# Reordering the opening and the first hand-over of a fused attention and MLP kernel on one Trainium2 core

## The chip, the core and the metric

The kernel runs on one core of one Trainium2 chip. The metric is device time in microseconds (us). Profiles are single executions; "span" is the profiled time from first to last instruction, some 2 us less than the timed figure. Every run here was in the fast state. A verdict compares the mean of one kernel's fast runs with the mean of the other's of the same rounds; that ratio is given with its 95% interval and is not quite the ratio of the medians also quoted. In the profiles PE is TensorE, DVE VectorE, ACT ScalarE, POOL GpSimd and SP SyncE.

## The reference, cut to what matters

```python
# attention part: batch 4, 8 heads, 768 positions, head dim 32, state 16, chunks
y_intra = einsum('bhij,bhjd->bhid', (C @ B.T) * exp(cum_i - cum_j) * causal, x)
y_inter = einsum('bhin,bhnd->bhid', C, state) * exp(cum_i)
state   = decay_full * state + sum_j(B_j x_j * decay_from_j)
# MLP part: 3072 tokens, 256 -> 2048 -> 256
h = y @ w_in ; g = h * clip(h + 3, 0, 6) / 6 ; out = g @ w_out
```

The kernel works in six chunks of 128 positions. The opening computes chunk 0's attention output. Chunk 0's MLP (the first MLP, writing `h`, then the output products, writing `o`) is followed by five denser stages. The weights arrive in a raw 64-bit form and are decoded by ScalarE and VectorE in eight parts, most of them while the first MLP runs.

Some names recur. `cb`, the scores, is the product of C and B; `bT` is B transposed and `csT` is C transposed and scaled; the state sum adds a chunk to the state, and the middle state (`mid`) stands between the chunk's two halves. The hand-over is the passage from chunk 0's output products to the next stage, and the lead is that stage's first products, put ahead of the rest.

## The kernel before

Each name is an instruction stream per engine; a call appends to all of them in program order. In the trace each engine's instructions follow in that order (PE, kernel before: C's transposes at 9.79 us, B's at 12.61, scores at 13.91, state sum at 16.47, products at 18.16).

```python
def turn_ps(c, j):                       # banks for the transposes of C (j=0), B (j=1)
    if c + j == 1: return ps.tile(..., tag="f1")
    if c * j == 1: return ps.tile(..., tag="f2")
    return ps_o.tile(..., tag="o")
def first_eto():
    e_ps = ps.tile([P, NB, HT], FP32, name="e_ps", tag="f0")   # ...
def scores(c):                           # C B^T into cb (f0..f3), then the state sum
    # ... 32 cb matmuls
    for b in range(NB):
        for q in range(NQ):
            for a in range(2):           # both halves of the state sum, at once
                nc.tensor.matmul(out=sps[c][a][...], ...)
def multiply(c):
    nc.scalar.copy(out=adds[c], in_=sps[c][1])
    for q in range(NQ):
        nc.vector.tensor_tensor(out=Ls[c]..., in0=Ls[c]..., in1=cbs[c][q], op=ALU.mult)
        if q == 1: ...                   # the middle state, from sps[c][0]
# a buffer of the MLP stages shares its tag with the output copy 'ob':
up = ffn.tile([P, 2, 2 * P], FP32, name="up", tag="ob", bufs=2)

# opening, in program order (cut)
diff(0, *range(NB)); load_w(1); load_w(2)
weights(0, ...)                          # decode of weight part 0
store_rows(); first_eto(); diff(1, 2, 3)
turn_c(0, t_ps); weights(0, 1); turn_b(0); fade_c(0, t_ps)
diff(1, 1); scores(0); diff_mask(1, 0); diff(1, 0)
multiply(0); mix(0)                      # mix: chunk 0's products, then from_state
by_token(); keep(0); weights(1, 2); renew(0); weights(1, 3)
# first MLP, then first_out(b, i): 16 units of 8 recorded PE products; (i, b) =
#   (2, 1): scores(1), multiply(1), renew(1)   (3, 0): results(1)   (3, 2): lead(1, 0)
```

## Time and profile before

| | value |
|---|---|
| time, median of 3 runs | 366.31 us |
| span of the profiled run | 364.3 us |
| PE busy | 347.9 us (96%) |
| PE idle in the opening (10 to 26 us) | 2.2 + 1.4 + 4.0 us |
| clock at half | 22.08 to 28.91 us |
| first MLP product / first output product | 25.75 / 54.87 us |

A line of a timeline has the start, the time to the group's end, engine and source line, what is written from what, shapes, the count, and in brackets the idle time ahead and what ended it; "issue" means that the profile shows nothing that was waited for. The lines of the kernel before stand in the prediction.

### The profile page before, as it was taken

The page shows a single profiled execution, that of the slowest core. Times are in us where ns is not written, and L with a number is a line of the kernel's source. Part 1 is how long each engine was busy: PE and PEld are TensorE (multiplying, and loading weights), DVE is VectorE, ACT ScalarE, POOL GpSimd, SP SyncE. Part 2 cuts the span into 40 slices and gives each one's busy share as a digit, 9 for nine tenths or more (in the row PEclk, how much of TensorE's full clock was granted, in tenths as well). Part 3 has the DMA queues.
Part 4 walks back from the last instruction along what each step waited for, and adds up shares of the span by engine and source line. Part 5 has one row for each costly group of instructions (what it writes and reads, how often), then busy time and mean ns, then how long its engine had stood idle before and what let it go on. Part 6 is the DMA issues. An engine that isn't in the chain of part 4 may idle for free.

```text
span 364.3 us, 9338 instructions
## 1 busy us (share of the span) xinstructions
PE 347.9 (96%) x3936; PEld 299.5 (82%) x3936; DVE 222.7 (61%) x429; ACT 176.2 (48%) x386; POOL 136.6 (38%) x138
## 2 busy tenths in 40 slices
PE   6659999989999999999999999999999999999996
PEld 2444448878788999888999888999888999888996
DVE  7729999976588625588436488435488411588111
ACT  5528888457556470376380376380367110376100
POOL 3200000072198922069822059820058800058800
PEclk9979999999999999999999999999999999999999
DMA  9975989900845025451016452000000000000000
GB/s 168 158 282 154 112 267 162 172 3 31 180 61 78 5 60 119 69 87 19 2 40 139 69 87 19 2 4 31 29 2 1 2 4 31 30 3 0 2 29 31
DMA packets 78538, 24.97 MB, mean 69 GB/s; under 512 B 69088, under 2 KB 74880, under 8 KB 77984
## 3 DMA queue, kind: packets, MB, share of 16 engines
q1 hardware_dynamic: 78496, 24.37, 36.0%
q8 instruction: 31, 0.51, 0.6%
q14 instruction: 11, 0.09, 0.1%
HBM read 21.07 MB, written 3.29 MB: 67 GB/s over the span
## 4 chain that ended last, share of the span: by engine, by line
PE 86%; DVE 4%; DMA 3%; ACT 2%; issue 2%; SPq 2%; DVEq 0%; ACTq 0%
PE ob L721 18%; PE oa L721 17%; PE even L610 16%; PE odd L610 12%; PE h L568 8%; PE o L662 7%; DMA xt<-in_x_dram 3%; PE y L546 3%; PE y L462 2%; SPq L92 1%; PE cb L485 1%; PE y L493 1%; DVE odd L639 1%; DMA out_dram<-ob 1%; DVE up L626 1%
## 5 line engine op out<-in xcount | busy, mean ns | idle before, releaser
L707 POOL TENSOR_TENSOR s<-gT 128x512 f32<-128x512 f32 x20 | 26.4, 1321 | 90.6 <-DVE gT L651 90.6
L610 PE MATMUL even<-ts,w_sum 128*128 128x256 f32 x160 | 48.3, 384 | 0.0
L625 ACT COPY even<-odd 128x512 f32<-128x512 f32 x40 | 23.1, 576 | 48.5 <-PE odd L610 46.3
L646 ACT ACTIVATE gT<-odd,half 128x512 f32<-128x512 f32 x40 | 27.5, 687 | 36.4 <-DVE odd L639 36.4
L610 PE MATMUL odd<-yT,w_in 128*128 128x256 f32 x160 | 41.1, 379 | 0.0
L721 PE MATMUL oa<-w_out,gT 128*128 128x128 f32 x320 | 38.9, 277 | 0.0
L721 PEld LDWEIGHTS oa<-w_out,gT 128*128 128x128 f32 x320 | 38.1, 192 | 0.9
L721 PE MATMUL ob<-w_out,s 128*128 128x128 f32 x320 | 37.4, 275 | 0.0
L721 PEld LDWEIGHTS ob<-w_out,s 128*128 128x128 f32 x320 | 36.5, 192 | 0.0
L610 PEld LDWEIGHTS even<-ts,w_sum 128*128 128x128 f32 x160 | 29.8, 190 | 5.5 <-ACT up L632 1.8
L651 DVE SCALAR_TENSOR_TENSOR gT<-gT,odd 128x512 f32<-128x512 f32 x40 | 27.5, 687 | 9.9 <-ACT gT L646 9.8
L610 PEld LDWEIGHTS odd<-yT,w_in 128*128 128x128 f32 x160 | 30.1, 190 | 3.9
L361 ACT ACTIVATE L<-L,cum_n 128x64 f32<-128x64 f32 x128 | 31.2, 339 | 0.0
L626 DVE COPY up<-odd 128x256 f32<-128x256 f32 x40 | 17.0, 424 | 22.1 <-ACT even L625 17.7
L721 PE MATMUL ob<-t,gT 128*128 128x128 f32 x240 | 30.3, 279 | 0.0
L646 ACT ACTIVATE gT<-even,half 128x512 f32<-128x512 f32 x40 | 27.7, 693 | 4.4 <-PE even L610 4.4
L651 DVE SCALAR_TENSOR_TENSOR gT<-gT,even 128x512 f32<-128x512 f32 x40 | 27.1, 678 | 4.4 <-ACT gT L646 4.4
L568 PE MATMUL h<-yT,w_in 128*128 128x512 f32 x64 | 29.3, 620 | 0.0
L721 PEld LDWEIGHTS ob<-t,gT 128*128 128x128 f32 x240 | 27.9, 192 | 1.1 <-issue 0.5
L662 PE MATMUL o<-w_out,gT 128*128 128x256 f32 x128 | 28.7, 381 | 0.0
L662 PEld LDWEIGHTS o<-w_out,gT 128*128 128x128 f32 x128 | 24.1, 190 | 3.7 <-issue 0.5
L379 POOL TENSOR_TENSOR tmp<-state,eto 128x256 f32<-128x256 f32 x5 | 3.1, 621 | 64.1 <-ACT eto L365 64.0
(126 smaller groups left out, 618.0 us busy)
## 6 DMA issues: line engine op xcount, KB each, us to landing
raw<-in_moe_w_in_dram SPq DMA_DIRECT2D x4, 1024.0 KB
raw<-in_moe_w_out_dram SPq DMA_DIRECT2D x4, 1024.0 KB
L<-cum_d SPq DMA_DIRECT2D x8, 512.0 KB
xt<-in_x_dram SPq DMA_DIRECT2D x6, 512.0 KB
out_dram<-res SPq DMA_DIRECT2D x20, 128.0 KB
B<-in_B_dram SPq DMA_DIRECT2D x6, 256.0 KB
eto<-cum_e SPq DMA_DIRECT2D x20, 64.0 KB
C<-in_C_dram SPq DMA_DIRECT2D x3, 256.0 KB
```

The costliest lines, as they stand in the source:

```text
L361: nc.scalar.activation(Ls[c][:, b, h], Ls[c][:, b, h], AF.Exp, bias=cum_n[:, c, g:g + 1])
L462: nc.tensor.matmul(out=ys[c][a, q // 2][d0:d0 + 2 * D, b], lhsT=state[pair, b], rhs=csT[pair, b, HALF[a]], start=(a == 0 and b == 0), stop ...
L546: nc.tensor.matmul(out=ys[c][a, u][d0:d0 + D, b], lhsT=xt[rows, b * NH + h], rhs=Ls[c][rows, b, h], start=(a == 1 and b == 0), stop=True, ...
L568: nc.tensor.matmul(out=h.rearrange("p r i -> p (r i)"), lhsT=w_in[:, j, f * P:(f + 1) * P], rhs=yTs[k][:, j].rearrange("p b i -> p (b i)") ...
L610: nc.tensor.matmul(out=bank[:, r], lhsT=lhsT, rhs=rhs, start=start, stop=True, skip_group_check=True)
L625: nc.scalar.copy(out=even, in_=odd[:, 1:2].to_broadcast([P, 2, 2 * P]))
L626: nc.vector.tensor_copy(out=up[:, 1], in_=odd[:, 0])
L646: nc.scalar.activation(gTs[k][:, f], h.rearrange("p r i -> p (r i)"), AF.Relu, bias=half, scale=1.0 / 6.0)
L651: nc.vector.scalar_tensor_tensor(out=g, in0=g, scalar=1.0, in1=h.rearrange("p r i -> p (r i)"), op0=ALU.min, op1=ALU.mult)
L662: nc.tensor.matmul(out=o[:, b % 2], lhsT=gTs[0][:, f, b * P:(b + 1) * P], rhs=w_out[:, f], start=(f == 0 and b % 2 == 0), stop=True, skip_ ...
L707: nc.gpsimd.tensor_tensor(out=o, in0=p_, in1=q_, op=op)
L721: nc.tensor.matmul(out=bank[:, slot], lhsT=lhs[:, j], rhs=rhs[:, j], start=(clear and j == 0), stop=True, skip_group_check=True)
```

## The change

It has two intents. In the opening, PE's wait for B is to be filled with chunk 1's differences and with idle products meant to keep the clock up, and half of the state sum goes behind the products so that they can start sooner. At the hand-over, chunk 1's scan moves one output unit on to cover a wait.

```diff
-        e_ps = ps.tile([P, NB, HT], FP32, name="e_ps", tag="f0")
+        e_ps = ps.tile([P, NB, HT], FP32, name="e_ps", tag="f1")
-        if c + j == 1: ...  # and the f2 case
+        if c < 2:
+            return ps.tile([P, NB, P], FP32, name="t_ps", tag=f"f{2 * j}")
+    def busy(n, bank):
+        for _ in range(n):
+            nc.tensor.matmul(out=bank..., lhsT=ident, rhs=ident...to_broadcast([P, NB, P]), ...)
         # scores:
+        if c == 0:
+            busy(1, both[1]...)
+            into_state(c, 0)
+        else:
+            into_state(c, 0, 1)
         # multiply: no copy of the second half for c == 0, and
-            if q == 1:
+            if q == (1 if c else NQ - 1):
-name="up", tag="ob", bufs=2)
+name="up", bufs=2)
     # opening
+    t_ps = turn_ps(0, 0)
     turn_c(0, t_ps)
+    diff(1, 0, 1)
+    busy(2, ps.tile([P, NB * P], FP32, name="d", tag="f3"))
     weights(0, 1)
     turn_b(0)
-    diff(1, 1)
     scores(0)
-    diff_mask(1, 0)
-    diff(1, 0)
     multiply(0)
     mix(0)
+    sps[0][1] = ps.tile([P, NB, 2 * D], FP32, name="sp", tag="f2")
+    into_state(0, 1)
     by_token()
     keep(0)
+    take(0)
     # not shown: the order of the masks and the start flag of the products
     # output units (cut): scores, multiply, renew from (2, 1) to (2, 2);
     # results from (3, 0) to (3, 1); lead from (3, 2) to (3, 3)
```

More of the change, by code (lines that the diff above doesn't have):

```diff
@@ L390, in turn_ps @@
     def turn_ps(c, j):
-        if c + j == 1:
-            return ps.tile([P, NB, P], FP32, name="t_ps", tag="f1")
-        if c * j == 1:
-            return ps.tile([P, NB, P], FP32, name="t_ps", tag="f2")
+        if c < 2:
+            return ps.tile([P, NB, P], FP32, name="t_ps", tag=f"f{2 * j}")
         return ps_o.tile([P, NB, P], FP32, name="t_ps", tag="o")
@@ L454, in turn_all @@
         nc.vector.tensor_tensor(out=csT, in0=csT, in1=etos[c], op=ALU.mult)
+    def busy(n, bank):
+        for _ in range(n):
+            nc.tensor.matmul(
+                out=bank.rearrange("p (b i) -> p b i", b=NB), lhsT=ident,
+                rhs=ident.unsqueeze(1).to_broadcast([P, NB, P]), start=True, stop=True)
     def from_state(c, a):
@@ L473, in scores @@
         bT, cT, _ = bTs[c]
-        xt, bs = xts[c], bss[c]
         cbs[c] = [ps.tile([P, NB, 2, HT], FP32, name="cb", tag=f"f{q}") for q in range(NQ)]
@@ L488, in scores, with into_state @@
                         tile_position=(32 * q, a * HT), skip_group_check=True)
+        if c == 0:
+            busy(1, both[1].rearrange("p k b i -> p (k b i)"))
+            into_state(c, 0)
+        else:
+            into_state(c, 0, 1)
+    def into_state(c, *halves):
+        xt, bs = xts[c], bss[c]
         for b in range(NB):
@@ L491, in scores @@
                 hs = slice(b * NH + 2 * q, b * NH + 2 * q + 2)
-                for a in range(2):
+                for a in halves:
                     nc.tensor.matmul(
@@ L505, in new_state, with take, multiply @@
                 in1=old[:, :, ds_], op0=ALU.mult, op1=ALU.add)
-    def multiply(c):
+    def take(c):
         adds[c] = att.tile([P, NB, 2 * D], FP32, name="adds", bufs=1)
         nc.scalar.copy(out=adds[c], in_=sps[c][1])
+    def multiply(c):
+        if c:
+            take(c)
         for q in range(NQ):
@@ L547, in mix @@
                             out=ys[c][a, u][d0:d0 + D, b], lhsT=xt[rows, b * NH + h],
-                            rhs=Ls[c][rows, b, h], start=(a == 1 and b == 0), stop=True,
+                            rhs=Ls[c][rows, b, h], start=(b == 0 and a >= min(c, 1)), stop=True,
                             tile_position=(a * HT, d0), skip_group_check=True)
@@ L621, in lead @@
         evens[k, s] = even = pool_e.tile([P, 2, 2 * P], FP32, name="even", tag=tag_e)
-        parts_of[k, s] = up = ffn.tile([P, 2, 2 * P], FP32, name="up", tag="ob", bufs=2)
+        parts_of[k, s] = up = ffn.tile([P, 2, 2 * P], FP32, name="up", bufs=2)
         half_product(odd, 1, wi[:, 0, 0, s], y_half(k, 0, 0), start=True)
@@ L803, in diff @@
                 part(c, b)
-    t_ps = turn_ps(0, 0)
-    for b in range(NB):
-        diff_mask(0, b)
-    for b in range(1, NB):
-        diff_mask(1, b)
+    for c in range(2):
+        for b in range(NB):
+            diff_mask(c, b)
     for sl in ends_at:
@@ L889 @@
                     elif (i, b) == (2, 1):
+                        next(sums_in)
+                    elif (i, b) == (2, 2):
                         scores(c)
@@ L892 @@
                         renew(c)
-                        next(sums_in)
-                    elif (i, b) == (2, 2):
                         decay_ends(ahead, 0)
                         next(sums)
+                    elif (i, b) == (2, 3):
                         next(sums)
-                    elif (i, b) == (2, 3):
                         decay_ends(ahead, 1)
                     elif (i, b) == (3, 0):
-                        results(c)
                         next(sums)
@@ L904 @@
                     elif (i, b) == (3, 1):
+                        results(c)
                         decay_ends(ahead, 3)
                         from_start(ahead)
-                    elif (i, b) == (3, 2):
+                    elif (i, b) == (3, 3):
                         lead(c, 0)
```

## The prediction

> **What bounds the kernel now.** I read the page's slices first: they say where the TensorE is not the bound. Then the timeline of PE and the one-microsecond windows of the opening, then the chain of waits around the hand-over from chunk 0 to chunk 1.
>
> The page's section 2 (40 slices, 9.1 us each):
>
> ```profile
> PE   6659999989999999999999999999999999999996
> ...
> PEclk9979999999999999999999999999999999999999
> ```
>
> The reader is to see that PE is at 9 everywhere except in the first three slices, in the one at 85-95 us, and at the very end; and that the third slice, 18-27 us, also has a lower clock. Of the 364.3 us span PE is busy 347.9, so at most 16.4 us can be won by filling gaps; some 10.9 of these lie before 26 us and 3 in the last output transfer, which the change does not touch.
>
> The timeline of PE from 10 to 26 us (start, time until the group's end, line, what it writes, count, idle time and what ended it):
>
> ```profile
> 12.61 0.63 PE L400 MATMUL t_ps<-ident,B 128*128 128x128 f32 x4 [2.16 <-DMA B<-in_B_dram]
> ...
> 13.91 1.21 PE L485 MATMUL cb<-cT,bT 32*64 32x128 f32 x64
> 16.47 0.85 PE L493 MATMUL y<-xt,bs 64*32 64x64 f32 x64 [1.36 <-DMA xt<-in_x_dram]
> ...
> 18.16 0.87 PE L546 MATMUL y<-L,xt 64*32 64x64 f32 x65
> 23.03 1.17 PE L546 MATMUL y<-L,xt 64*32 64x64 f32 x63 [4.00 <-issue]
> ```
>
> Three holes: 2.2 us for B, 1.4 us for x, and 4.0 us in the middle of chunk 0's products that no semaphore explains ("issue"). That last one is the largest hole of the kernel. I believe it is an instruction fetch: the DMA section has 31 packets of 16 KB on an "instruction" queue; one starts at 20.69 us and takes 1.03, and PE goes on at 23.03, 1.3 us after its end. Counting recorded PE instructions, the stall comes after number 705. If every 256 form a block, the edges lie at 193, 449, 705, ..., and number 3009 is one too: there PE shows another hole marked "issue" (0.25 us, ending at 133.93), again 1.33 us after the end of an instruction packet (132.60). That is a good check of the idea. PE passed edge 449 at 16.60 us; the packet then asked for waited 4.1 us, while in quiet stretches such packets start 0.6 to 1.0 us after the edge. The windows show why:
>
> ```profile
> 18.00:19.00 1.00, 1.00 (x81) 0.88 (x74) 0.96 (x2) 0.00 (x0) 0.00 (x0) 1.00 1.02 418
> 20.00:21.00 1.00, 0.00 (x0) 0.00 (x0) 0.00 (x0) 0.00 (x0) 0.00 (x0) 1.00 1.09 438
> 22.00:23.00 1.00, 0.00 (x0) 0.00 (x0) 0.00 (x0) 0.00 (x0) 0.00 (x0) 0.54 1.02 414
> ```
>
> The last three columns are clock, DMA share and GB/s: three weight loads of 1 MB run from 15.6 to 24.5 us at over 400 GB/s, and all five engines stand still. The clock then is half from 22.08 to 28.91 us.
>
> Two more holes matter, at 73-74 and 94-95 us (PE's and VectorE's waits in order of time):
>
> ```profile
> 74.10 0.62 PE L462 MATMUL y<-csT,state 32*64 32x64 f32 x25 [0.92 <-DVE csT L426]
> ```
> ```profile
> 94.07 0.42 DVE L626 COPY up<-odd 128x256 f32<-128x256 f32 x1 [3.64 <-DMA out_dram<-ob]
> ```
> ```profile
> 95.43 0.70 PE L610 MATMUL even<-yT,w_sum 128*128 128x256 f32 x2 [0.75 <-DVE odd L639]
> ```
>
> [...] Here it stayed half for 6.83 us[...], after a 4.2 us hole, and kept full speed through the holes of 2.2 and 1.4 us. So the idle matmuls in those two holes have little clock to save.
>
> **The change part by part: opening.** Moving chunk 0's C transposes to bank f0 pushes the small decay product (e_ps) to f1, which ScalarE frees one exponential later: 8.95 for 8.44 us, so e_ps at 9.0 instead of 8.5, C's transposes end near 10.95 (10.45), and C's scaling on VectorE, which leads a queue with 0.7 + 1.36 + 0.41 us behind it, makes csT final at 14.9 (14.44). Chunk 1's differences for b = 0 and 1 (34 instruction pairs, 1.2 us by the same group at 8.63-9.85) now fill PE up to 12.1. The two idle fp32 matmuls are two passes of 0.43 us each (as L568's), 1.72 us: to 13.8. B's transposes, possible at 12.6, so come 1.2 us late. That is where the fill is too long. bT is copied by 15.1 and the scores run 15.15-16.1 instead of 13.91-14.85. Half of this comes back: the wait for x is over by then, half of the state sum (32 pairs) and 0.4 + 0.44 us of differences leave the path, and VectorE's four multiplications need no state sum in their middle: 16.4 + 4 x 0.64 = 19.0 us against 18.95 before. Without a fetch stall the products would end at 19.85, from_state at 20.6, and the MLP would start at 21.2 instead of 25.75.
>
> But the stall: in the new order I count 18 instructions to the masks' end, 306 after the differences, 322 after B's transposes, 450 after the scores, 518 after half the state sum, 774 after the products. Edge 449 is thus passed at 16.0 instead of 16.6, and edge 705 again lies inside the products, reached at 19.4. The fetch probably still meets the weight loads. With the same 6.43 us from edge to resumption PE resumes at 22.4; 69 product instructions, from_state, the moved state sum and the transposes follow, 1.9 us at full clock: MLP at 24.3. The hole is 3.0 us[...]. VectorE is 7.8 of 8 us busy from 26 to 42 us, and its decode chain starts with ScalarE's copy, 25.56 before and about 24.4 now: 1.15 earlier. The tightest weight part was ready 0.59 us before its use (54.28 for 54.87), so PE gains at most 1.15 + 0.59 = 1.7 us. With the clock halved, 0.4. If the fetch waits for one packet less, near 3; if it isn't delayed at all, 4.3 + 0.6 = 4.9. I weigh these 0.30, 0.35 (half clock or no gain at all), 0.20, 0.15 and get about 1.9 us.
>
> **Hand-over to chunk 1.** Scores one unit (8 instructions, 1.72 us) later: the 0.92 us wait for csT is covered. The lead moves to directly ahead of stage 1; its first product must be copied by ScalarE (0.58 us) behind the last output copy (0.57) before PE may go on: about 0.5 us of new wait. So even's first matmul comes at 89.45 for 90.08, 0.6 us earlier. "up" gets buffers of its own, so VectorE no longer waits 3.64 us for the output transfer, and PE's hole of 0.75 goes. Sum 1.4 us, and I take 1.2.
>
> From there PE is dense, so a gain made is kept: 366.31 - 1.9 - 1.2 = 363.2 us.
>
> **Rivals.** (a) The fetch lands early enough and the 4 us vanish: for it, the instructions moved ahead put edge 449 at the end of the scores, where before it lay 41 instructions behind them, beyond the wait for x; against it, the scores are themselves 1.2 us late[...]. Some 360.1 us. (b) The stall stays as long as it was, resuming at 23.0 with half clock, and only the hand-over counts: 365. For it: the packet may be served at a fixed point between loads. (c) VectorE becomes the bound in the first MLP, being 97% busy there: caps the gain as above. (d) The longer fill makes B late and the opening slower: at worst +0.5 us.
>
> **Range and chances.** (a) at its best with everything from the hand-over gives 360.0, (b) with a poor hand-over 365.6: I take 360.3 to 365.6. For 2% the time would have to be under 359.0, which even (a) does not reach: 0.04. Slower by 2% needs a new stall: 0.01.
>
> **What would show it.** PE's B transposes near 13.8 us; scores near 15.2; a hole marked "issue" in the products beginning near 19.4 and shorter than 4 us, with an instruction packet 1.3 us before its end; the first MLP matmul between 24 and 25 us; no wait at chunk 1's from_state; no VectorE wait on an output transfer; a short PE wait for ScalarE after the lead. Wrong would be: no hole at all (my count of edges or the arrival order is off), the hole moved to the MLP, or VectorE's decode holding PE in the first MLP by more than 1 us.

How long the fetch would wait behind the loads and whether the clock would fall were the author's estimates; neither was shown when the forecast was made.

## The result

The changed kernel took 365.31 us (365.08 to 365.55, 4 runs) beside 366.14 for the kernel before: ratio 0.9975 [0.9958, 0.9993]. Timed again later in a larger call it was 365.9 beside 365.71: 1.0004 [0.9988, 1.002]. So the two timings give a gain of 0.8 us and none, where 3.1 was forecast.

The changed kernel's 40 slices, PE's busy share and its clock:

```profile
PE   6859999999999999999999999999999999999996
...
PEclk9978999999999999999999999999999999999999
```

The slice that stood at 8 before (the ninth, 72.9 to 82.0 us) is filled. In the opening the second slice went from 6 to 8, the third stayed at 5, and the clock is a tenth lower in the fourth. The changed kernel's timeline of PE in the opening:

```profile
12.11 1.98 PE L457 MATMUL d<-ident 128*128 128x512 f32 x4
13.93 0.60 PE L398 MATMUL t_ps<-ident,B 128*128 128x128 f32 x4
15.21 1.21 PE L489 MATMUL cb<-cT,bT 32*64 32x128 f32 x64 [0.67 <-ACT bT L407]
16.35 1.12 PE L457 MATMUL y<-ident 128*128 128x512 f32 x2
17.40 0.65 PE L505 MATMUL y<-xt,bs 64*32 64x64 f32 x32
19.35 1.14 PE L562 MATMUL y<-L,xt 64*32 64x64 f32 x92 [1.30 <-DVE mid L536]
23.50 0.85 PE L562 MATMUL y<-L,xt 64*32 64x64 f32 x36 [3.01 <-issue]
24.28 1.13 PE L467 MATMUL y<-csT,mid 32*64 32x64 f32 x32
25.34 1.08 PE L505 MATMUL sp<-xt,bs 64*32 64x64 f32 x32
26.35 0.63 PE L300 MATMUL c_ps<-ident,pre 32*128 32x32 f32 x4
26.91 5.61 PE L584 MATMUL h<-yT,w_in 128*128 128x512 f32 x9
```

The waits for B and x are gone, filled. In their place is a 1.30 us wait for the middle state, and the hole marked "issue" is still there. It is shorter only because it begins later. It ends at 23.50 us for 23.03, and the MLP begins at 26.91 for 25.75. The hand-over, PE in the same kernel:

```profile
75.92 0.61 PE L467 MATMUL y<-csT,state 32*64 32x64 f32 x25
...
89.31 1.03 PE L626 MATMUL odd<-yT,w_in 128*128 128x256 f32 x4
91.06 0.70 PE L626 MATMUL even<-yT,w_in 128*128 128x256 f32 x2 [0.71 <-ACT even L641]
```

The wait for csT (0.92 us) and that of VectorE on the output transfer (3.64 us) have gone, and a new one of 0.71 us stands behind the lead. From the first output product to the first product of stage 1's output (`oa`) the kernel before took 61.22 us (54.87 to 116.09) and the changed one 59.96 (55.96 to 115.92). So in this pair of profiles the opening lost 1.1 us and the hand-over won 1.3.

### The profile page after: what moved, and what is told of

Read it like the earlier page. It is cut to its first block, busy times and chain, and to the rows that moved or that the text cites. A ratio compares the mean times of both kernels' runs of the same rounds, so it can differ in the third digit from the quotient of the medians.

```text
span 363.8 us, 9347 instructions
## 1 busy us (share of the span) xinstructions
PE 351.1 (97%) x3942; PEld 301.2 (83%) x3942; DVE 226.0 (62%) x429; ACT 176.0 (48%) x386; POOL 138.6 (38%) x138
## 4 chain that ended last, share of the span: by engine, by line
PE 88%; SPq 3%; DVE 3%; DMA 2%; ACT 2%; issue 1%; DVEq 0%; ACTq 0%
PE ob L737 18%; PE oa L737 17%; PE even L626 16%; PE odd L626 12%; PE h L584 8%; PE o L678 8%; PE y L562 3%; SPq L99 2%; PE y L467 2%; PE cb L489 2%; DMA raw<-in_moe_w_in_dram 2%; PE y L505 1%; DVE L L529 1%; SPq L291 1%; DMA pairs<-in_C_dram 1%
## 5 line engine op out<-in xcount | busy, mean ns | idle before, releaser
L723 POOL TENSOR_TENSOR s<-gT 128x512 f32<-128x512 f32 x20 | 26.4, 1322 | 91.2 <-DVE gT L667 91.2
```

The source lines that it names most:

```text
L723: nc.gpsimd.tensor_tensor(out=o, in0=p_, in1=q_, op=op)
```

## The experiments

Eighteen runs were made, all correct; three of them repeat a kernel. Two theories stood at first. (1) The hand-over is worth what was forecast and the opening lost it again, because PE waits for an instruction fetch behind the weight loads. (2) The opening is neutral and the hand-over is worth only the 0.8 us seen, the later MLP being scatter of one profile.

| kernel | median us | ratio to before, 95% |
|---|---|---|
| opening_only | 367.41 | 1.0036 [1.0022, 1.0051] |
| handover_only / handover_again | 364.79 / 364.50 | 0.9969 [0.9956, 0.9982] / 0.9962 [0.9952, 0.9972] |
| up_only | 364.26 | 0.9957 [0.9944, 0.9970] |
| order_only | 364.84 | 0.9967 [0.9953, 0.9981] |
| lead_early | 364.61 | 0.9954 [0.9937, 0.9972] |
| no_idle | 365.76 | 0.9988 [0.9976, 1.0000] |
| state_front / state_front_again | 365.14 / 365.23 | 0.9970 [0.9956, 0.9985] / 0.9979 [0.9965, 0.9993] |
| sum_behind | 365.67 | 0.9986 [0.9970, 1.0003] |
| after_again | 365.90 | 1.0004 [0.9988, 1.0020] |
| held_loads | 366.41 | 1.0009 [1.0000, 1.0018] |
| pad60 / pad60_hoist | 370.74 / 370.09 | 1.0119 [1.0096, 1.0141] / 1.0111 [1.0081, 1.0142] |
| hoist | 363.70 | 0.9929 [0.9902, 0.9956] |
| held23_hoist | 362.63 | 0.9907 [0.9891, 0.9923] |
| best | 362.76 | 0.9913 [0.9890, 0.9935] |
| after_held | 363.21 | 0.9920 [0.9897, 0.9943] |

### The two halves of the change

**opening_only** is the changed kernel with the hand-over undone:

```diff
-name="up", bufs=2)
+name="up", tag="ob", bufs=2)
 # and the output units' order as before
```

> The changed kernel with the loop of chunk 0's output products and the 'up' buffers as before: only the opening's part. Theory (the opening lost what the hand-over won): slower than before by 0.5 to 1.2 us; the first MLP matmul at 26.3 to 27.0 us for 25.75; an 'issue' hole of about 3 us in the products, half clock after it. Rival (the later MLP start in the changed kernel's one profile is scatter of the first loads, which landed 0.6 us later there): within 0.3 us of before.

Slower by 0.36%, some 1.3 us; theory 1. In its profile the MLP began at 25.84, hardly later than before and under the forecast, but the first output product came at 55.70 for 54.87: the clock was at half until 30.47, for 28.91 before.

**handover_only** is the kernel before with the order of output units and the `up` tag of the change.

> The kernel before with only the loop order of the hand-over and the own buffers of 'up'. Theory: faster than before by 1.3 to 2.0 us, no wait for csT before chunk 1's from_state and none of VectorE on an output transfer. Rival (opening neutral, hand-over worth only what the whole change showed): faster by 0.6 to 1.0 us.

Faster by 0.31%, 1.1 us: between the two theories, so it decides little by itself.

**after_again** and **handover_again** are the changed kernel and the hand-over alone, unedited, timed together because the two differences above did not add up well.

> The changed kernel, unedited, timed with the hand-over alone on one chip. Theory (the opening costs: 0.6 us more behind the fetch hole, clock half for as long): -0.1 to -0.3% against before, 0.4 to 1.2 us slower than the hand-over alone. Rival (opening neutral): within 0.3 us of it.

> The hand-over alone, unedited, again. Theory: -0.3 to -0.45% against before. Rival (opening neutral): level with the changed kernel.

On one chip the changed kernel was level with before and the hand-over 0.38% faster. The opening costs some 0.4% (1.5 us), as it does alone, and theory 2 fell. The changed kernel's first timing (0.9975), set against the hand-over's two, would give only 0.2 to 0.5 us, but it comes from another call.

### The parts of the hand-over

**up_only**:

```diff
-name="up", tag="ob", bufs=2)
+name="up", bufs=2)
```

> The kernel before with own buffers for 'up' and nothing else. Theory: the 3.6 us wait of VectorE and the 0.75 us hole of PE at 94 us go, faster by 0.4 to 0.9 us, and the 0.92 us wait for csT stays. Rival: the hole is only put off (the pair of ScalarE and VectorE work behind it needs the time anyway): within 0.3 us.

Faster by 0.43%, above the range. VectorE's wait on the output transfer is gone, and so is PE's 0.75 us hole; first output product to `oa` fell from 61.22 to 60.10 us.

**order_only** has the order alone, with the shared buffers.

> The kernel before with only the loop order of the hand-over ('up' still shares buffers with the output copy). Theory from own 'up' buffers alone at -0.43% and both together at -0.31%: the order covers the 0.92 us wait for csT and pays 0.7 us for ScalarE's copy behind the lead, so within 0.5 us of before. Rival (each half is worth what I predicted): faster by 0.5 to 1 us.

Faster by 0.33%, more than expected: 59.96 us from the first output product to `oa`. Its trace has no wait on the output transfer either, probably because with the lead behind the last output unit the second `up` comes after the transfers. So the order and the buffers both remove the same hole, and either gives most of what both give: the terms were not to be added.

**lead_early** puts the lead one unit ahead again:

```diff
-                    elif (i, b) == (3, 3):
+                    elif (i, b) == (3, 2):
                         lead(c, 0)
```

> Own 'up' buffers and the loop order, but the lead left one unit ahead, after the third unit of the last round. Theory (the copy behind the lead is what gave the 0.92 us back): the 0.7 us hole at stage 1's first product of 'even' shrinks to under 0.3 us, 0.4 to 0.9 us faster than with the lead moved, so 0.5 to 0.7% under before. Rival (the sums of y or ScalarE's queue aren't ready then): the hole moves to the lead, no gain.

The rival happened: the hole moved into the lead, whose second product waits 1.10 us for the sums of y (PE, lead_early):

```profile
86.24 0.59 PE L610 MATMUL odd<-yT,w_in 128*128 128x256 f32 x2
87.94 0.70 PE L610 MATMUL odd<-yT,w_in 128*128 128x256 f32 x2 [1.10 <-DVE yT L607]
```

Its time, 0.9954, is not told from the others'.

### What the 4 us hole is

**held_loads**:

```diff
-    load_w(1)
-    load_w(2)
 ...
-    store_rows()
 ...
     multiply(0)
+    gate_d = dram.tile([16, 2 * D], FP32, name="gate_d")
+    nc.sync.dma_start(out=gate_d, in_=adds[0][:16, 0])
+    for i in range(1, NRAW + 1):      # weight loads 1 to 3
+        load_w(i)
+    store_rows()
     mix(0)
```

> The kernel before, but weight loads 1 to 3 are held back on the DMA queue behind a 4 KB transfer that reads chunk 0's copied state sum (ready at 17.4 us), so that they run from about 19 us instead of 15.6. Theory (the 4 us hole is an instruction fetch that waits behind 4 KB packets): the instruction packet starts about 18.5 for 20.7, the hole after instruction 705 falls to 0.5 to 1.8 us, no half clock, the MLP starts at 21.8 to 23.2 us, and the kernel is 1.5 to 4 us faster. Rival (the hole has another cause, or the fetch is served at a fixed time): hole still 3.5 to 4.5 us, the same or slower by up to 1 us as the weights come later.

The hole behaved as the theory says, and the time did not (PE, held_loads):

```profile
18.36 0.87 PE L546 MATMUL y<-L,xt 64*32 64x64 f32 x65
20.49 0.84 PE L546 MATMUL y<-L,xt 64*32 64x64 f32 x63 [1.26 <-issue]
...
22.42 7.22 PE L568 MATMUL h<-yT,w_in 128*128 128x512 f32 x16
32.62 1.22 PE L568 MATMUL h<-yT,w_in 128*128 128x512 f32 x1 [2.98 <-DVE gT L651]
```

The instruction packet started at 17.78 us instead of 20.69, the hole fell from 4.0 to 1.26 us and the MLP began 3.3 us earlier. So the cause of the hole is shown. Then PE stood 2.98 us for VectorE's product at 31.88 us, which waited for ScalarE (held_loads):

```profile
31.16 0.69 ACT L646 ACTIVATE gT<-h,half 128x512 f32<-128x512 f32 x1 [2.93 <-DMA cum_d<-pre]
```

ScalarE waited for a store. The edit puts `store_rows` behind the loads too, and `pre`, which it reads, shares its buffer with `gT` (`pre = ffn.tile(..., name="pre", tag="gT")`). The decode of part 1 ended at 30.90 us and PE stopped at 29.64, so the held load alone would have cost some 1.3 us (an estimate from these two times); the rest of the wait is of the edit's own making. What an earlier MLP is worth by itself this run does not show.

The table gathers the packet that the hole waits for, by kernel. Edge 449 is the end of the block of 256 PE instructions before the one at whose end the hole stands (see the prediction). The block's size is a reading of the trace of the kernel before: 31 instruction packets of 16,384 bytes stand beside 7,911 PE instructions, 255 for each packet, and after nine of the edges, 1,473 to 6,593, a packet starts 0.63 to 1.00 us behind the edge. At other edges the count fits less closely. The packet is taken to be asked for at the edge; the trace does not show the asking. "Packets before" counts the 4 KB packets of the weight loads started before it (256 for a load of 1 MB), divided by the 16 DMA engines that the page counts.

| kernel | PE passes edge 449 | weight loads begin | packet starts | packets before | PE resumes |
|---|---|---|---|---|---|
| before | 16.60 | 15.57 | 20.69 | 27.3 | 23.03 |
| up_only | 16.53 | 15.34 | 20.46 | 27.2 | 22.90 |
| changed | 16.13 | 16.12 | 21.03 | 26.0 | 23.50 |
| opening_only | 15.95 | 15.57 | 20.58 | 26.8 | 22.86 |
| changed (after_again) | 16.01 | 15.40 | 20.38 | 26.1 | 22.73 |
| no_idle | 16.55 | 15.40 | 20.35 | 25.9 | 22.68 |
| held_loads | 16.80 | 20.08 | 17.78 | 0 | 20.49 |
| pad60_hoist | 14.63 | 15.49 | 15.39 | 0 | no hole |
| held23_hoist | 16.60 | 15.58 | 18.91 | 15.7 | 21.22 |
| best | 16.66 | 15.62 | 19.20 | 15.8 | 21.67 |

With three loads queued the packet started after 25.9 to 27.3 of their packets in the six rows that have them, whether PE passed the edge at 15.95 or at 16.6 us. Where no load had begun it went 0.98 us (held_loads) and 0.76 us (pad60_hoist) after the edge. Six more runs with three loads queued, not in the table, have 25.7 to 26.4. The spread was larger in three others: 23.9 in handover_only, 19.8 in pad60 (which passed the edge at 15.49 us) and 30.8 in state_front_again.

**pad60** moves the edges without touching the loads:

```diff
+    for _ in range(60):
+        nc.tensor.matmul(out=t_ps[:32, 0, :8], lhsT=ident_h[:, :32], rhs=ident_h[:, :8],
+                         start=True, stop=True)
     for sl in ends_at:
         log_a(sl)
```

> The kernel before with own 'up' buffers and 60 tiny bf16 products (32 columns loaded, 8 streamed, into a bank that is overwritten later) in PE's wait at 4.6 to 6.4 us: they only move the edges of the 256-instruction blocks by 120 instructions. Theory (a fetch asked for before the weight loads begin at 15.6 us is served in about 1.2 us, one asked for during them at a fixed place, after some 26 of their 4 KB packets per engine): the first edge is passed by 14.3 us, that packet starts before 16 us and costs no hole; the next edge's packet starts near 20.5, and the hole moves to the last 60 instructions ahead of the MLP, which starts at 23.2 to 24.2 us; but the time gains only 0 to 1.5 us on own 'up' buffers alone, since the weight decode starts late. Rival (the hole is not tied to the instruction count): hole at the same product as before, MLP at 25 to 26 us, slower by the tiny products.

4.4 us slower; the gain predicted for it failed. B came late in its profiled run and edge 449 was passed at 15.49 us, too late to be ahead of the loads. There are two holes in its opening, the second of them 256 instructions after the first, and three more behind stage 2 that only pad60_hoist, with the same pads, has as well (PE, pad60):

```profile
21.89 1.80 PE L546 MATMUL y<-L,xt 64*32 64x64 f32 x122 [2.27 <-issue]
...
26.82 1.11 PE L462 MATMUL y<-csT,mid 32*64 32x64 f32 x27 [2.73 <-issue]
```
```profile
182.15 0.30 PE L493 MATMUL y<-xt,bs 64*32 64x64 f32 x4 [0.73 <-issue]
```
```profile
302.94 0.45 PE L462 MATMUL y<-csT,mid 32*64 32x64 f32 x12 [1.14 <-issue]
```

The three later holes make 2.6 of the 4.8 us by which its span is longer than before. That these holes follow the instruction count is thereby shown, and in pad60 the place of the edges cost time behind stage 2 as well as in the opening. In this respect the kernel before was already well placed: its only other such hole was 0.25 us.

**hoist**, on up_only:

```diff
     mix(0)
+    weights(1, 3)
     by_token()
     keep(0)
-    weights(1, 2)
     renew(0)
-    weights(1, 3)
+    weights(1, 2)
```

> The kernel before with own 'up' buffers, and the first three steps of weight part 1's decode put ahead of the copies of chunk 0's result, so that ScalarE and VectorE do them in the hole at 19 to 25 us. Theory (before, PE and not the decode is what the first MLP waits for): decode of part 1 ends 2.5 to 5 us earlier, the same MLP start, time within 0.6 us of own 'up' buffers alone. Rival (decode is the bound there): faster by 1 us or more than that.

0.9929 against 0.9957 for up_only, in different calls and with overlapping intervals: up to 1 us better, not settled. The decode's start moved as meant (19.65 us for 24.91), its end only from 31.55 to 30.70, since the later steps still stand behind the copies of chunk 0's result.

**pad60_hoist** is both.

> Both of the above. Theory (PE's start and the decode must come earlier together): MLP at 23.2 to 24.2 us without a wait for weights, and 1.5 to 3 us faster than own 'up' buffers alone (some 361.5 to 363). Rival (half clock or VectorE eats it): within 0.6 us of the better of the two.

As slow as pad60. Its profile has the first packet ahead of the loads (15.39 us) and no hole where the others have theirs; but the next edge, passed at 18.50 us, came into the loads, and its hole, on the second line, is 4.31 us (PE, pad60_hoist):

```profile
18.10 1.86 PE L546 MATMUL y<-L,xt 64*32 64x64 f32 x128
...
24.53 1.11 PE L462 MATMUL y<-csT,mid 32*64 32x64 f32 x27 [4.31 <-issue]
...
181.08 0.30 PE L493 MATMUL y<-xt,bs 64*32 64x64 f32 x4 [1.50 <-issue]
```

The opening accounts for little of the loss: the MLP began at 26.13 us for 25.75 before. The last line is the first of three later holes, 1.50, 0.75 and 0.85 us at the same instruction counts as pad60's. Together they are 3.1 us, and its span is 3.4 us longer than before.

**held23_hoist**, on up_only with the hoist, holds back loads 2 and 3 only:

```diff
     load_w(1)
-    load_w(2)
 ...
-    store_rows()
 ...
     multiply(0)
+    gate_d = dram.tile([16, 2 * D], FP32, name="gate_d")
+    nc.sync.dma_start(out=gate_d, in_=adds[0][:16, 0])
+    load_w(2)
+    load_w(3)
+    store_rows()
     mix(0)
```

> Own 'up' buffers, weight part 1's first decode steps hoisted into the hole, and only weight loads 2 and 3 held back behind the 4 KB transfer at 17.4 us, load 1 at its old time. Theory (the fetch waits for what is queued ahead of it): the instruction packet starts when load 1 ends, 18.3 to 19.3 us, PE resumes at 20.7 to 21.7, MLP at 23.0 to 24.2, decode of part 1 done before 31, and 1 to 2.5 us faster than own 'up' buffers alone (361.8 to 363.3). Rival (the fetch's time is fixed by something else): packet still at 20.4 us, no gain.

The forecast held: 362.63 us, 0.93% under before. With one load queued the packet waited for that one's 15.7 packets per engine and no more (PE, held23_hoist):

```profile
18.15 0.87 PE L546 MATMUL y<-L,xt 64*32 64x64 f32 x65
21.22 0.84 PE L546 MATMUL y<-L,xt 64*32 64x64 f32 x63 [2.20 <-issue]
22.00 0.69 PE L462 MATMUL y<-csT,mid 32*64 32x64 f32 x32
22.62 0.43 PE L300 MATMUL c_ps<-ident,pre 32*128 32x32 f32 x4
23.15 4.22 PE L568 MATMUL h<-yT,w_in 128*128 128x512 f32 x9
...
38.09 1.12 PE L568 MATMUL h<-yT,w_in 128*128 128x512 f32 x2 [0.71 <-DVE w_in L219]
```

The hole of 2.2 us did not cost the clock in this run (its mean was 1.000), so the way from resumption to the MLP took 1.9 us instead of 2.7. PE now waits for VectorE's decode, 0.71 us at weight part 2 and 0.36 at part 3. That does not show that the decode has become the bound, as the prediction's rival (c) has it: here too ScalarE's first activation waited for the moved store (4.47 us, until 28.62), and its first step of part 2's decode came behind it, at 29.20. In best, below, the same loads were held, no such wait shows, and PE waited for no weights, though its MLP began 1.1 us later and partly at half clock. The two edits together gain clearly on up_only (0.9957), but against hoist alone (0.9929) the intervals overlap, so the held loads' own share is not settled.

**best** adds the order of the hand-over to held23_hoist; **after_held** is the whole change with the same two edits, the held loads waiting for the second product of the decays.

> Hand-over as changed (order and 'up'), opening as before, with weight loads 2 and 3 held back and the decode's first steps hoisted. Theory: as the same without the loop order (-0.93%), or up to 0.3 us better as csT's wait is covered and the lead's copy costs 0.7: 362.3 to 363.2 us. Packet at 18.5 to 19.2 us, resumption near 21.2, full clock from 10 us on.

> The changed kernel with weight loads 2 and 3 held back (behind a 4 KB transfer that reads the second product of the decays, ready near 17.7 us) and the decode's first steps hoisted. Theory (its own longer path keeps it behind: scores 1.2 us later, the moved state sum behind the hole): packet near 19, resumption near 21.2, hole under 1.5 us, MLP at 23.3 to 24.3, and 0.3 to 1.2 us slower than best. Rival (only the fetch kept the opening from paying): level with best or faster.

Both beat the two kernels of this study, and they are level with each other and with held23_hoist. After_held came out as the rival said: with the fetch served early (its packet started at 18.97 us, and PE had no hole marked "issue" in the opening) the change's opening cost nothing that shows; nor did it win. Its MLP began at 23.51 us, held23_hoist's at 23.15 and best's at 24.27. For best, full clock was forecast and missed: its profile is at half from 21.91 to 28.74 us, and four of its six runs had a mean clock of 0.991. All six of after_held, whose profile has no such hole, had 1.000.

### Which part of the opening costs

**no_idle** is the changed kernel without its three idle products.

> The changed kernel without its three idle products, 12 instructions and 2.6 us of PE fewer. Theory (they delay B's transposes by 1.2 us, and the clock falls after the fetch hole all the same): transposes of B at 12.6 to 13.0, scores at 14.3 to 14.6 us, and within 0.5 us of the changed kernel or up to 0.8 us faster, as the resumption is fixed by the loads. Rival (the idle products save clock): half clock appears ahead of 20 us, and it is slower than the changed kernel by 0.5 us or more.

0.9988: between the changed kernel's two timings. The time shows no use of the idle products, and the clock shows that they do what they are meant to. Three-microsecond windows (columns: window, length, busy time and count of PE, weight loads, VectorE, ScalarE and GpSimd, then granted clock, DMA share, GB/s) of the changed kernel and of no_idle:

```profile
18.00:21.00 3.00, 1.19 (x96) 0.98 (x93) 1.29 (x3) 0.37 (x1) 0.00 (x0) 1.00 1.03 419
21.00:24.00 3.00, 0.50 (x35) 0.50 (x35) 0.00 (x0) 0.00 (x0) 0.00 (x0) 0.85 1.02 411
24.00:27.00 3.00, 3.00 (x88) 2.48 (x72) 0.00 (x0) 0.89 (x3) 0.00 (x0) 0.50 0.41 133
```
```profile
18.00:21.00 3.00, 1.46 (x98) 1.46 (x98) 1.49 (x3) 0.25 (x1) 0.00 (x0) 0.50 1.02 416
21.00:24.00 3.00, 1.56 (x71) 1.15 (x61) 0.00 (x0) 0.12 (x1) 0.00 (x0) 0.50 1.02 402
24.00:27.00 3.00, 3.00 (x54) 2.06 (x49) 0.98 (x4) 1.75 (x3) 0.00 (x0) 0.50 0.19 53
```

Without them the clock is at half from 15.42 to 29.07 us, 13.65 us long, and in all 22 timed runs the mean granted clock was 0.981 or 0.986, where 12 of 14 runs of the changed kernel had 0.991. But the added half-clock time lies where PE waits for the fetch anyway. The half-clock period that costs, the one behind the hole, both have.

**state_front** and **state_front_again** are the changed kernel with both halves of the state sum ahead of the products:

```diff
         if c == 0:
             busy(1, both[1]...)
-            into_state(c, 0)
-        else:
-            into_state(c, 0, 1)
+        into_state(c, 0, 1)
```

> The changed kernel with both halves of chunk 0's state sum ahead of the products again, as before, idle products kept. Theory (the resumption after the hole is fixed by the weight loads, and what stands behind it is paid in full, at half clock): hole begins a little later and ends at the same 22.9 to 23.5 us, half a state sum (1.0 us at half clock) fewer behind it, MLP at 25.3 to 26.0, and 0.5 to 1.2 us faster than the changed kernel. Rival (the moved sum is paid nowhere): same as the changed kernel or slower.

> The changed kernel with both halves of the state sum ahead of the products, again, for the same chip. Theory (the later scores are hidden by the fetch hole, so the fill costs little): -0.25 to -0.4% against before, and 0.3 us or more ahead of the state sum behind. Rival (the fill is what costs): 0 to -0.15%, and behind it.

**sum_behind** has the hand-over and, of the opening, only the moved half of the state sum with the later middle state.

> The hand-over as changed, and of the opening only the state sum's second half behind the products and the middle state after all four multiplications. Theory (what stands behind the fetch hole is paid in full at half clock): hole ends at 22.5 to 23.1 as in the kernel before, 3.0 to 3.4 us from there to the MLP instead of 2.7, -0.1 to -0.3% against before (0.4 to 1 us slower than the hand-over's -0.31 and -0.38%). Rival (it costs nothing; the fill ahead of B's transposes does): -0.3 to -0.4%.

In one call, 0.9979 and 0.9986: by its mean each of the two parts alone lies between the hand-over (0.9962 and 0.9969) and the whole change timed again (1.0004); the intervals overlap, and the two are not told apart. State_front's first timing, 0.9970, is level with the hand-over. The moved sum puts 1.08 us of half-clock products behind the hole, and the middle state behind all four multiplications keeps the products waiting (1.30 us in the changed kernel): they write the tile from which VectorE reads that state, and the trace puts their wait down to this read. The fill delays the scores, to 15.5 us on average in the six profiles that have all of it from 14.2 in the eleven with neither it nor pads. How the cost divides stays open.

A rival was not tested. In the profiles with all three loads queued, the first output product roughly follows the end of the half-clock period, whatever the opening: 27.36 and 53.80 us in up_only, 28.91 and 54.87 before, 29.93 and 55.96 in the changed kernel, but also 30.56 and 55.63 in handover_again, which has the old opening. The new opening's hole begins later (20.30 to 20.49 us for 18.83 to 19.14), so part of its cost may be that the clock falls later and more of the half-clock time lies in the MLP.

## Why the prediction was wrong

The forecast was 363.2 us, 3.1 us won; 0.8 and, the second time, nothing was measured. The first timing lies inside the stated range, near its upper end, and the second just above it.

- **What bounds the opening**: right. The hole is an instruction fetch behind the weight loads; held_loads, the pads and held23_hoist show it (4.00 us before, 1.26 in held_loads, 2.20 in held23_hoist).
- **The step that failed** is "With the same 6.43 us from edge to resumption PE resumes at 22.4". The wait was not counted from the edge. With three loads queued the packet started after some 26 packets per engine wherever PE passed the edge between 15.95 and 16.7 us: PE resumed at 22.73 to 23.50 us in the three profiles with the whole opening, at 22.59 to 23.14 in the six with the opening as before that had neither pads, held loads nor the hoist. Passing the edge 0.5 to 0.7 us earlier (16.13, 16.01 and 15.95 for 16.60) was worth nothing. Rival (b) had it right and got too little weight. That the hole was 3.01 us long where 3.0 was forecast is luck: it began and ended 1.1 us later than forecast.
- **The term behind it was mis-sized**: "1.9 us at full clock" from resumption to the MLP measured 3.41, 3.06 and 2.98 in those three (changed, after_again, opening_only; 2.2 to 2.7 with the old opening). It ran wholly at half clock in the first, and from some 0.75 us after the resumption in the other two. The moved half of the state sum takes 1.08 us there; both halves together took 0.85 at full clock before. Weighting the half clock as one case among several, which was the author's estimate, was wrong: 12 of 14 runs of the changed kernel in the second timing had a mean clock of 0.991, as its profile with a 6.8 us half-clock period has.
- **A wait that was missed**: the prediction has the products under way and at edge 705 by 19.4 us; they wait for the middle state until 19.35, and the hole begins at 20.49. The hole hides this wait.
- **The cap by the decode**: not settled. PE waits for weights in held23_hoist and after_held (0.71 + 0.36 us each), where a moved store had delayed ScalarE, and not in best, hoist or the changed kernel.
- **The idle products**: "have little clock to save" was wrong for this opening. Without them the clock fell at 15.42 us (no_idle). Yet the time shows no gain from them.
- **Two readings**: the slice with the dip is at 72.9 to 82.0 us, not 85 to 95, and the hole ahead of the half clock is 4.0 us, not 4.2. Neither carries the forecast.
- **The fill is too long**: right. B's transposes were predicted near 13.8 and came at 13.93; scores predicted 15.15, measured 15.21.
- **The hand-over**: the sum was right (1.2 taken, 1.26 us measured between `o` and `oa`, 1.1 to 1.4 us timed), but by luck, for its parts were not: order and buffers remove the same hole, and the lead's new wait is 0.71 us rather than 0.5.

So the change moved little because one half gave back what the other won: the opening costs 1.3 to 1.5 us in the two comparisons within one call, the hand-over gains 1.1 to 1.4.

## What to carry to other kernels

A hole that no semaphore explains may be the instruction stream. Count the engine's instructions to it, look for the instruction packet that lands just ahead of its end (by 1.31 us in the kernel before), and see which large loads were queued when the edge was passed; then hold back loads that nobody needs yet, rather than shorten the work in front. Before filling a wait with work, look at which wait ends last behind it, since here everything saved ahead of the fetch was lost in it; and don't add up two repairs before asking if they remove the same hole. When an experiment moves a load, look at what else it moved: here a store behind the loads held a buffer, and its wait looked like that for the weights.

## The fetch, the loads and the clock in these runs

- Holes marked "issue" were 1.44 us (no_idle) to 4.31 us (pad60_hoist) long in the opening where loads were queued ahead of the packet, 1.26 us in held_loads where none was, and 0.73 to 1.50 us behind stage 2 in the two kernels with pads. Pad60's 60 tiny products move the edges by 120 instructions; it was 4.4 us slower on the whole. PE went on 1.31 us after the packet's end in the kernel before and 1.43 us in the changed one.
- PE ran dry 256 instructions after the edge behind which the packet came: it passed edge 449 at 16.60 us and stopped at 705, its work done at 19.03 us, in the kernel before.
- With one load of 1 MB queued the packet waited for 15.7 (held23_hoist) and 15.8 (best) of the load's 16 packets of 4 KB per engine, and with three for 19.8 to 30.8 of 48, mostly 26.
- Half-clock periods were 6.83 us (22.08 to 28.91 before, 23.10 to 29.93 in the changed kernel) and 13.65 us (no_idle). In the kernel before the clock fell at 22.08 us; PE had been busy for 0.03 us of the stretch from 19 to 22 us. In no_idle it was at half from 24 to 27 us, though PE was busy for all 3.00 us, with small products until 25.91. What makes it fall and rise was not shown.
